# Score products with zero-padded queries on the whole TensorE array, and q and k asked for two batches ahead, in a fused attention and MLP kernel

## Chip, core and metric

The kernel runs on one core of a Trainium2 chip. The metric is device time in microseconds (us) of one execution. Engines are named as in the profile: PE (TensorE matmul), PEld (TensorE weight load), DVE (VectorE), ACT (ScalarE), POOL (GpSimd) and SP (SyncE, which here only issues DMAs).

## The reference

Longformer-style attention (8 batches, 8 heads, 576 positions, head size 64, a band of 32 to each side and 8 global positions), followed by a two-layer MLP with a softplus:

```python
scores = scale * np.matmul(q, k.transpose(0, 1, 3, 2))          # q, k, v: (8, 8, 576, 64) float32
mask = np.abs(pos[:, None] - pos[None, :]) <= 32
mask = mask | is_global[:, None] | is_global[None, :]
scores = np.where(mask, scores, -1000000000.0)
scores = scores - np.max(scores, axis=-1, keepdims=True)
attn = np.exp(scores)
attn = attn / (np.sum(attn, axis=-1, keepdims=True) + 1e-09)
attn_out = np.matmul(attn, v)
x = attn_out.transpose(0, 2, 1, 3).reshape(4608, 512)
h = x @ w_in                                                    # (512, 2048)
g = np.maximum(h, 0.0) + np.log1p(np.exp(-np.abs(h)))
out = g @ w_out                                                 # (2048, 512)
```

## The kernel before

**Units.** Each batch's 576 rows are cut into nine blocks of 64 queries; a block of all eight heads is a *unit*, so there are 72 units. The heads go in four pairs: partitions 0 to 63 belong to the pair's first head, 64 to 127 to its second. For a unit the band needs 128 keys, and 8 global keys stand between them: 136 columns (`EXT`).

A unit's work: the score products (`sc`, L621) from the queries `qx` and the keys `kx` into a PSUM tile `s`, two head pairs to a tile; masking and row maximum on DVE (`top`, L627) into `st`; the exponential on ACT (`ex`, L648) into `pe`; row sum and reciprocal on DVE (`su`, L656 to L658) into `rs`; normalising on POOL (`no`, L664) into `pn`; transposes on PE (`tp`, L674) and their copy to `pt` by ACT or DVE. Four units make a group: `val` (L717, L724) multiplies by v into `xo`, which is copied into `xT`.

In `sc` a head pair is two matmuls, each on a 64 by 64 part of the array: head 0 on the rows and columns 0 to 63, head 1 on 64 to 127. The profile writes this as `64*64`; `128*128` is the whole array, and `72*64`, `72*32` and `128*32` are other parts.

**Batches.** For each batch q and k come by one casting DMA each from POOL's queue (`load_qk`, L220) into `qn` and `kn`, v by five DMAs from SP's queue (`load_v`, L212), each two-buffered by the batch's parity. POOL casts v to `vA`, and `shift` (L443, L444) copies it by DMA to `vB`, displaced by 64 rows. PE gathers the global rows (`pick`, L463) and transposes k and q (`tk`, L505; `tq`, L513); ACT or DVE copies each result (`kev` into `kx`, `qev` into `qx`). All of these copies are made in the helper `copy`, L409. The rows of the global queries have a small attention of their own (`sg`, `mx`, `gexp`, `tg`, `lge`, `ov`, `oz`).

**MLP tiles.** Eight units (512 tokens) make an MLP tile; there are nine. `first` (L759) gives 16 PSUM tiles `h`, ACT makes the softplus `g` of each (L764), and `second` (L769) accumulates four output tiles `o`. Exponential and softplus are in different ACT tables, so the work alternates: in an *h phase* PE makes h and ACT the softplus; in an *o phase* PE makes o, while the softmax of the next tile's units runs on DVE, ACT and POOL.

**The order.** All pieces of work are handed to a planner, `_Order` (L19), with a cost for each engine that may do them, and the work that they depend on. It simulates the engines, at each step takes the piece that can begin first (then by `rank`, then by number), picks the engine, and so fixes the order on each engine. Its costs are fixed numbers; PE's costs know nothing of a change between parts of the array. For loads it keeps a clock for each of the two DMA queues: `moves` ns after a start delay of 2000, and 1000 more. The instructions then go out in that order, and each engine executes its own in order.

`AHEAD` says how many units beyond its own a tile's o phase prepares. The load of q and k for batch b is put behind the normalising of unit 0 of batch b - 1 (`T["no", (b - 1) * NJ]`) and behind that batch's `shift`. `blank_q` (L269) zeroes the places of `kx` and `qg` that are never written: for buffer 0 right after the first q load on POOL, for buffer 1 as a planned piece.

Of the kernel before, what the change touches and what calls it, by code (L numbers as in the profile page):

```python
# [18 lines left out]
class _Order:  # L19
# [4 lines left out]
    HOP = 45  # L24

    def __init__(self, slots, kinds, banks):
        self.slots = slots
        self.kinds = kinds
        self.jobs = []
        self.opened = {p: [] for p in list(slots) + list(kinds)}  # L30
        self.users = {}
        self.banks = [None] * banks
        self.bank = {}

    def add(self, cost, emit, deps=(), rank=5, opens=(), uses=(), table=None, moves=0):

        job = dict(cost=cost, emit=emit, deps=[d for d in deps if d is not None], rank=rank, opens=list(opens),
                   table=table, moves=moves, n=len(self.jobs), at=None, end=None)
        self.jobs.append(job)
        for pool, key in job["opens"]:  # L40
            self.users.setdefault(key, []).append(job)
        for key in uses:
            self.users.setdefault(key, []).append(job)
        return job
# [30 lines left out]
    def run(self, free):  # L75
# [9 lines left out]
        order = []  # L85
        table = None
        dma = dict(SP=0, POOL=0)
        while ready:
            best = None
            for j in ready:  # L90
                t0 = max([d["at"] if d["on"] in j["cost"] and (
                    d["on"] == "PE" or d["on"] == "DMA" and (not d["moves"] or not j["moves"] and d["cost"]["DMA"][0]) or d["on"] == "POOL" and d["moves"]) else d["end"] + self.HOP
                          for d in j["deps"]] or [0])
                if j["opens"]:
                    t = self.room(j["opens"])
                    if t is None:
                        continue
                    t0 = max(t0, t)
                for e in j["cost"]:
                    t = max(t0, free[e])  # L100
                    key = (t, j["rank"], j["n"])
                    if best is None or key < best[0]:
                        best = key, j, e
            if best is None:
                raise ValueError("the order is stuck")
            _, j, e = best
            t = best[0][0]
            ready.remove(j)
            step, took = j["cost"][e]
            for pool, key in j["opens"]:  # L110
                self.opened[pool].append(key)
                if pool in self.kinds:
                    ends = [(self.closed(k), n) for n, k in enumerate(self.banks)]
                    n = min(x for x in ends if x[0] is not None)[1]
                    self.banks[n] = key
                    self.bank[key] = n
            if j["table"] and j["table"] != table:
                table = j["table"]
                t += 1290
            if j["moves"]:  # L120

                mine = "POOL" if "POOL" in j["cost"] or not j["cost"][e][0] else "SP"
                other = "SP" if mine == "POOL" else "POOL"
                start = max(dma[mine], t + 2000)
                shared = min(j["moves"], max(0, dma[other] - start))
                dma[mine] = start + j["moves"] + shared
                dma[other] += shared if dma[other] > start else 0
                j["at"], j["end"] = t, dma[mine] + 1000
            else:
                j["at"], j["end"] = t, t + took  # L130
            free[e] = t + step
            j["on"] = e
            order.append(j)
            for k in after.get(j["n"], ()):
                waiting[k["n"]] -= 1
                if waiting[k["n"]] == 0:
                    ready.append(k)
# [7 lines left out]
def kernel(  # L145
# [38 lines left out]
    SUMMED = 5  # L184
    AHEAD = [1, 2, 3, 3, 3, 3, 3, 3]

# [72 lines left out]

    qx = [const([P, HP, S], BF16, f"qx{i}") for i in range(2)]  # L260
    kx = [const([P, HP, NH5, W], BF16, f"kx{i}") for i in range(2)]
# [7 lines left out]
    def blank_q(i, eng):  # L269
        eng.memset(kx[i][:, :, 0, 0:WIN].bitcast(I32), 0)  # L270
        eng.memset(kx[i][:, :, NH5 - 1, G - WIN:G].bitcast(I32), 0)
        clear(eng, qg[i][:])

    mask = const([P, NJ, EXT], BF16, "mask")
# [127 lines left out]
    def pool(n):  # L402
        return {"POOL": (n, n)}
# [11 lines left out]
    def add_load(b, which, deps):  # L415
        if which == 2:
            T["load", b, 2] = [o.add({"DMA": (100, 0)}, lambda e, x=x: load_v(b, x), deps, rank=0,
                                     opens=[("in_v", ("in", b, 2, x))], moves=1200) for x in range(NT5)]
            return
        early = [T.get(("t" + "qk"[which], b - 2, p)) for p in range(HP)]  # L420
        early += [T.get(("pick", b - 2, x)) for x in range(2)]
        T["load", b, which] = [o.add({"POOL" if b else "DMA": (880 if b else 0, 0)},
                                     lambda e: load_qk(b, which) if b else None, deps + early, rank=0, moves=4300)]

    def add_cast(b, engines):
# [19 lines left out]
        T["shift", b] = o.add({"DMA": (100, 0)}, shift, T["cast", b, 2] + early, rank=0, moves=1500)  # L445

    def add_prep(b, gate, rank):
# [38 lines left out]
        for n, ws in enumerate(steps):  # L486
            T["pick", b, n] = o.add({"PE": (460 * len(ws) + 190, 460 * len(ws) + 300)}, lambda e, ws=ws: pick(e, ws),
                                    [T["load", b, w][0] for w in ws] + [T.get(("pick", b, n - 1))], rank=4,
                                    opens=[("pick", ("pick", b)), ("gk", ("gk", b))] if n == 0 else [],
# [10 lines left out]
        for p in range(HP):  # L500
# [24 lines left out]
            def qev(e, p=p):  # L525
                copy(e, qx[i][:, p, :].rearrange("c (q r) -> c q r", r=QR),
                     PS["tq", b, p][:].rearrange("c r q -> c q r"))
            T["tk", b, p] = o.add(mm(QR, NQ), tk, [T["load", b, 1][0], *gate], rank=rank, opens=[("tk", ("tk", b, p))])
            T["kev", b, p] = o.add({"ACT": (635, 720), "DVE": (800, 880)}, kev, [T["tk", b, p], *late, *blanks["g"]],
                                   rank=3, uses=[("tk", b, p)])  # L530
            T["tq", b, p] = o.add(mm(QR, NQ), tq, [T["load", b, 0][0], *gate], rank=rank, opens=[("tq", ("tq", b, p))])
            T["qev", b, p] = o.add({"ACT": (650, 740), "DVE": (675, 750)}, qev, [T["tq", b, p], *late], rank=3,
                                   uses=[("tq", b, p)])

    PARTS = ((0, 6, WIN, 6 * G), (6, 4, 0, 4 * G - WIN))

    def add_global(b, gate, early):
# [49 lines left out]
        def oze(e):  # L587
            for p in range(HP):
# [3 lines left out]
        ready = [T["kev", b, p] for p in range(HP)] + [T["gev", b]]  # L592
        T["sg", b] = o.add({"PE": (390, 600)}, sg, ready + early, rank=3,
                           opens=[("sg", ("sg", b, 0)), ("sg", ("sg", b, 1)), ("small", ("m2", b))])
# [6 lines left out]
                            [T["tg", b], T.get(("ov", b - 2)), T.get(("blank_g", b))], rank=2, uses=[("tg", b)])  # L601
        T["ov", b] = o.add({"PE": (393, 600)}, ov, [T["lge", b], *T["cast", b, 2], T.get(("ones_g", b))], rank=3, opens=[("ov", ("ov", b))])
        old = [T.get(("val", n4)) for n4 in range(NU)
# [4 lines left out]
    def add_scores(n, gate, rank):  # L608
# [3 lines left out]
        def sc(e, x):  # L612
# [5 lines left out]
            for y in range(2):  # L618
                for h in range(2):
                    r = slice(h * D, (h + 1) * D)  # L620
                    nc.tensor.matmul(out=ps[r, y, :], lhsT=qx[i][r, x * 2 + y, j * G:(j + 1) * G],  # L621
                                     rhs=kf[r, x * 2 + y, j * W:j * W + EXT], start=True, stop=True)

# [68 lines left out]
    def add_values(n4):  # L692
# [51 lines left out]
        T["val", n4] = o.add({"PE": (1030, 1190)}, val_, ready, rank=0,  # L744
                             opens=[("xo", ("xo", n4, half)) for half in range(2)] + ([("xT", ("xT", m))] if part == 0 else []),
# [81 lines left out]
    T["select"] = setup(select_rows, {"DVE": (1174, 1260)}, [T["places"]], 5)  # L827
    T["blank_q", 1] = setup(lambda: blank_q(1, nc.gpsimd), pool(700), [], 6)
    for i in range(2):
# [23 lines left out]
    def make_batch(b, gate, rank):  # L853
# [3 lines left out]
        if b > 1:  # L857
            for w in (1, 0):
                add_load(b, w, [T["no", (b - 1) * NJ], T["shift", b - 1]])
            add_load(b, 2, [T["shift", b - 1]])  # L860
# [27 lines left out]

    for job in o.run(dict(PE=5000, ACT=2000, DVE=4700, POOL=5800, DMA=1000)):
        job["emit"](job["on"])  # L890
# [28 lines left out]
```

## Time and profile before

Three runs gave 421.93, 424.46 and 427.48 us; the median is 424.46 us. The profile is of one execution of its own.

| | |
|---|---|
| time of the profiled execution | 427.72 us |
| its span, first to last instruction | 426.0 us |
| mean granted TensorE clock | 0.984 |
| PE busy | 390.6 us, 92%, 5440 matmuls |
| DVE busy | 246.4 us, 58% |
| ACT busy | 277.4 us, 65% |
| POOL busy | 142.3 us, 33% |
| score products L621 | 576 matmuls of 64 by 64, 39.0 us busy |
| copies of q, `qx<-tq` | 18 on DVE, mean 754 ns; 14 on ACT, mean 641 ns |
| q0 (POOL's loads), share of the 16 DMA engines | 21.6% |
| q1 (SP's transfers) | 21.3% |

A busy matmul row counts its passage through the array, so rows overlap and their sum says little. The step from the start of one row to the start of the next, on the PE timeline, says what a piece costs PE. "Idle before" names what the engine waited for.

### The profile page before, as it was taken

Reading aid. Unit: us, or ns where it says so; the run is one execution under the profiler, and the core shown is the slowest. Engines: PE = TensorE matmul, PEld = TensorE weight load, DVE = VectorE, ACT = ScalarE, POOL = GpSimd, SP = SyncE. Lnnn points to the kernel's source line nnn. Section 1 sums busy time; section 2 is a strip of 40 time slices with the busy share of each in tenths; the row PEclk is TensorE's granted clock in tenths of the full one; section 3 lists DMA queues with packets and bytes.
Section 4 is the critical chain, followed back from the end, with each engine's and each line's share of the span. In section 5 each row is a group of like instructions: output and inputs, shape, how many; then the busy total and the mean of one; then the engine's idle time right before and its main releaser. Section 6 shows DMA issues by size and latency. Waiting matters only on the chain.

```text
span 426.0 us, 13459 instructions
## 1 busy us (share of the span) xinstructions
PE 390.6 (92%) x5440; PEld 205.3 (48%) x5440; DVE 246.4 (58%) x1099; ACT 277.4 (65%) x669; POOL 142.3 (33%) x249
## 2 busy tenths in 40 slices
PE   1857998999998999789996999999989999999996
PEld 1635544554455445434543455545544555445442
DVE  5698338954587449711885168835874387425011
ACT  2787568854786667747765687668665887585620
POOL 7565605810086006700463004710471044014000
PEclk9999998999999999969999999999999999999999
DMA  6997997870078204940078101960182011001011
GB/s 94 167 221 107 166 193 127 173 165 2 26 129 200 47 0 83 211 85 2 26 143 171 37 2 55 180 142 2 52 149 66 2 51 54 0 24 53 2 49 74
DMA packets 59470, 37.57 MB, mean 88 GB/s; under 512 B 42001, under 2 KB 53265, under 8 KB 59409
## 3 DMA queue, kind: packets, MB, share of 16 engines
q0 software_dynamic: 15232, 13.65, 21.6%
q1 hardware_dynamic: 44176, 23.08, 21.3%
q8 instruction: 42, 0.69, 0.7%
q14 instruction: 20, 0.16, 0.1%
HBM read 36.71 MB, written 9.44 MB: 108 GB/s over the span
## 4 chain that ended last, share of the span: by engine, by line
PE 67%; DMA 14%; DVE 7%; ACT 5%; issue 3%; POOL 3%; SPq 0%; DVEq 0%; POOLq 0%; ACTq 0%
PE h L759 29%; PE o L769 20%; DMA qn<-in_q_dram 6%; DMA kn<-in_k_dram 6%; PE s L621 4%; PE tp L674 3%; ACT pe L648 2%; DVE sm L656 2%; PE tk L505 2%; PE tq L513 2%; PE pick L463 2%; POOL pn L664 2%; DMA v<-in_v_dram 1%; PE xo L717 1%; PE xo L724 1%
## 5 line engine op out<-in xcount | busy, mean ns | idle before, releaser
L664 POOL TENSOR_TENSOR pn<-pe,rs 128x512 bf16<-128x512 f32 x72 | 74.9, 1040 | 233.7 <-DVE rs L658 98.6
L769 PE MATMUL o<-wout,g 128*128 128x512 bf16 x576 | 144.7, 381 | 0.0
L759 PE MATMUL h<-xT,win 128*128 128x512 bf16 x576 | 136.9, 386 | 0.8 <-DVE xT L409 0.6
L764 ACT ACTIVATE g<-h 128x512 bf16<-128x512 f32 x144 | 84.6, 598 | 56.4 <-PE h L759 50.6
L648 ACT ACTIVATE pe<-st,nb 128x136 f32<-128x136 f32 x288 | 93.4, 398 | 9.4 <-POOL gw L668 4.0
L627 DVE CUSTOM_DVE_ANT_0 st<-s,mask 128x136 f32<-128x136 f32 x288 | 70.6, 294 | 32.5 <-PE s L621 32.0
L759 PEld LDWEIGHTS <-win 128*128 128x128 bf16 x576 | 53.7, 99 | 62.8 <-issue 4.8
L769 PEld LDWEIGHTS <-g 128*128 128x128 bf16 x576 | 50.8, 98 | 52.3 <-issue 2.0
L656 DVE TENSOR_REDUCE sm<-pe 128x4 f32<-128x544 f32 x67 | 47.7, 712 | 10.5 <-ACT pe L648 10.2
L621 PE MATMUL s<-kx,qx 64*64 64x136 bf16 x576 | 39.0, 243 | 1.1 <-DVE qx L409 0.6
L621 PEld LDWEIGHTS <-qx 64*64 64x64 bf16 x576 | 20.9, 113 | 32.5 <-issue 26.3
L674 PE MATMUL tp<-ident_b,pn 128*128 128x128 bf16 x288 | 30.0, 232 | 6.9 <-POOL pn L664 6.7
L436 POOL CAST vA<-v 128x512 bf16<-128x512 f32 (+3 forms) x48 | 28.6, 612 | 11.5 <-DMA v<-in_v_dram 8.9
L409 DVE COPY qx<-tq 128x576 bf16<-128x576 bf16 x18 | 13.4, 754 | 31.2 <-PE tq L513 30.9
L674 PEld LDWEIGHTS <-pn 128*128 128x128 bf16 x288 | 20.4, 102 | 20.8 <-POOL pn L664 11.9
L409 ACT COPY pt<-tp 128x512 bf16<-128x512 bf16 x32 | 18.7, 585 | 13.3 <-PE tp L674 13.3
L409 DVE COPY kx<-tk 128x32 bf16<-128x32 bf16 (+1 forms) x45 | 13.1, 349 | 23.4 <-PE tk L505 23.4
L409 DVE COPY osb<-o 128x512 f32<-128x512 f32 x11 | 7.6, 690 | 32.3 <-PE o L769 32.3
L409 ACT COPY osb<-o 128x512 f32<-128x512 f32 x25 | 14.6, 585 | 16.6 <-PE o L769 12.5
L627 DVE DVE_READ_ACCUMULATOR2_ANT nb<- 128x1 f32 x288 | 23.7, 82 | 0.0
L409 DVE COPY pt<-tp 128x512 bf16<-128x512 bf16 x40 | 16.8, 421 | 11.3 <-PE tp L674 10.9
L658 DVE TENSOR_SCALAR rs<-rs,notg 128x4 f32<-128x4 f32 x72 | 19.6, 272 | 2.6
(118 smaller groups left out, 400.1 us busy)
## 6 DMA issues: line engine op xcount, KB each, us to landing
out_dram<-osb SPq DMA_DIRECT2D x36, 256.0 KB, 2.2
v<-in_v_dram SPq DMA_DIRECT2D x24, 256.0 KB, 6.1
kn<-in_k_dram POOLq DMA_DIRECT2D x8, 576.0 KB, 8.2
qn<-in_q_dram POOLq DMA_DIRECT2D x8, 576.0 KB, 12.4
vB<-vA SPq DMA_DIRECT2D x16, 256.0 KB, 4.7
v<-in_v_dram SPq DMA_DIRECT2D x16, 192.0 KB, 4.8
win<-in_moe_w_in_dram POOLq DMA_DIRECT2D x4, 512.0 KB, 9.8
wout<-in_moe_w_out_dram POOLq DMA_DIRECT2D x4, 512.0 KB, 12.1
```

The costliest lines, as they stand in the source:

```text
L409: (nc.scalar.copy if e == "ACT" else nc.vector.tensor_copy)(out, in_)
L436: nc.gpsimd.tensor_copy(to[r], at[r])
L621: nc.tensor.matmul(out=ps[r, y, :], lhsT=qx[i][r, x * 2 + y, j * G:(j + 1) * G], rhs=kf[r, x * 2 + y, j * W:j * W + EXT], start=True, stop ...
L627: nc.vector.tensor_tensor_reduce(out=PS["st", n][:, p, :], in0=PS["s", n, x][:, y, :], in1=mask[:, j, :], scale=-SCALE, scalar=3.0e38, op0 ...
L648: nc.scalar.activation(out=pe[:, p, 0:EXT], in_=PS["st", n][:, p, :], func=AF.Exp, bias=PS["nb", n][:, p:p + 1], scale=-1.0, **({"accum_ou ...
L656: nc.vector.reduce_sum(out=sm[:], in_=PS["pe", n][:, :, 0:EXT], axis=AX)
L658: nc.vector.tensor_scalar(out=rs[:], in0=rs[:], scalar1=notg[:, j:j + 1], scalar2=None, op0=OP.mult)
L664: nc.gpsimd.tensor_tensor(out=pn[:].rearrange("c p (a s) -> c p a s", a=2), in0=wide[:, :, :, 0:G], in1=rs[:].unsqueeze(2).unsqueeze(3).to ...
L674: nc.tensor.transpose(out=ps[:, p, :], in_=PS["pn", n][:, p, :], identity=ident_b[:])
L759: nc.tensor.matmul(out=h[:, :], lhsT=w_in_t[kd][:, c * P:(c + 1) * P], rhs=PS["xT", m][:, kd, :], start=(kd == 0), stop=(kd == KD - 1))
L764: nc.scalar.activation(out=t[:, :], in_=PS["h", m, c][:, :], func=AF.Softplus)
L769: nc.tensor.matmul(out=PS["o", m, ns][:, :], lhsT=PS["g", m, kf][:, ns * P:(ns + 1) * P], rhs=w_out_t[kf // 4][:, kf % 4, :], start=(kf == ...
```

## The change

1. **Score products.** `qx` becomes `qz`, with 128 columns for each block and head pair: head 0's 64 queries (zero on partitions 64 to 127), then head 1's 64 queries (zero on partitions 0 to 63). A head pair is then one matmul of the whole array with the same 136 columns: 288 instead of 576 matmuls.
2. **Copies of q.** `qev` writes the two halves separately, 64 partitions each, one instruction after the other on the same engine. Its planned cost is doubled. The zeros are written once: eight more memsets in each `blank_q`.
3. **Loads.** q and k of batch b are put behind the normalising of unit 2 of batch b - 2 instead of unit 0 of batch b - 1; the dependence on the `shift` of batch b - 1 stays. From batch 2 on, the planner takes loads and shifts to land 2 to 4 us later (`slack`).
4. **The planner's PE costs.** Jobs on a part of the array are marked `tiled` (no longer the score products); a change into or out of a part costs 95 ns.
5. **`AHEAD`** is 4 instead of 3 from the fourth tile on. POOL's start in the plan is 8300 instead of 5800.

```diff
+    SWITCH = 95
...
-                    t = max(t0, free[e])
+                    t = max(t0, free[e] + (self.SWITCH if e == "PE" and tiled and not j["tiled"] else 0))
...
+            if e == "PE":
+                if j["tiled"] and not tiled:
+                    t += self.SWITCH
+                tiled = j["tiled"]
...
-                j["at"], j["end"] = t, dma[mine] + 1000
+                j["at"], j["end"] = t, dma[mine] + 1000 + j["slack"]
...
-    AHEAD = [1, 2, 3, 3, 3, 3, 3, 3]
+    AHEAD = [1, 2, 3, 4, 4, 4, 4, 4]
...
-    qx = [const([P, HP, S], BF16, f"qx{i}") for i in range(2)]
+    qz = [const([P, HP, NJ, 2, G], BF16, f"qz{i}") for i in range(2)]
...
+        for p in range(HP):
+            eng.memset(qz[i][0:D, p, :, 1, :].bitcast(I32), 0)
+            eng.memset(qz[i][D:P, p, :, 0, :].bitcast(I32), 0)
...
-                                     lambda e: load_qk(b, which) if b else None, deps + early, rank=0, moves=4300)]
+                                     lambda e: load_qk(b, which) if b else None, deps + early, rank=0, moves=4300, slack=4000 if b > 1 else 0)]
...
-                copy(e, qx[i][:, p, :].rearrange("c (q r) -> c q r", r=QR),
-                     PS["tq", b, p][:].rearrange("c r q -> c q r"))
+                for h in range(2):
+                    r = slice(h * D, (h + 1) * D)
+                    copy(e, qz[i][r, p, :, h, :].rearrange("c j (q r) -> c j q r", r=QR),
+                         PS["tq", b, p][r].rearrange("c r (j q) -> c j q r", j=NJ))
...
-            T["qev", b, p] = o.add({"ACT": (650, 740), "DVE": (675, 750)}, qev, [T["tq", b, p], *late], rank=3,
+            T["qev", b, p] = o.add({"ACT": (1290, 1390), "DVE": (1350, 1430)}, qev, [T["tq", b, p], *late, *blanks["q"]], rank=3,
...
-                for h in range(2):
-                    r = slice(h * D, (h + 1) * D)
-                    nc.tensor.matmul(out=ps[r, y, :], lhsT=qx[i][r, x * 2 + y, j * G:(j + 1) * G],
-                                     rhs=kf[r, x * 2 + y, j * W:j * W + EXT], start=True, stop=True)
+                nc.tensor.matmul(out=ps[:, y, :], lhsT=qz[i][:, x * 2 + y, j, :, :],
+                                 rhs=kf[:, x * 2 + y, j * W:j * W + EXT], start=True, stop=True)
...
-                add_load(b, w, [T["no", (b - 1) * NJ], T["shift", b - 1]])
+                add_load(b, w, [T["no", (b - 2) * NJ + 2], T["shift", b - 1]])
...
-    for job in o.run(dict(PE=5000, ACT=2000, DVE=4700, POOL=5800, DMA=1000)):
+    for job in o.run(dict(PE=5000, ACT=2000, DVE=4700, POOL=8300, DMA=1000)):
```

Marked `tiled=True`: `pick`, `tk`, `tq`, `sg`, `ov` and `val`. The v loads get a slack of 3000 and `shift` one of 2000, from batch 2 on.

More of the change, by code (lines that the diff above doesn't have):

```diff
@@ L33, in __init__, with add @@
         self.bank = {}
-    def add(self, cost, emit, deps=(), rank=5, opens=(), uses=(), table=None, moves=0):
+    def add(self, cost, emit, deps=(), rank=5, opens=(), uses=(), table=None, moves=0, tiled=False, slack=0):
         job = dict(cost=cost, emit=emit, deps=[d for d in deps if d is not None], rank=rank, opens=list(opens),
-                   table=table, moves=moves, n=len(self.jobs), at=None, end=None)
+                   table=table, moves=moves, tiled=tiled, slack=slack, n=len(self.jobs), at=None, end=None)
         self.jobs.append(job)
@@ L86, in run @@
         table = None
+        tiled = False
         dma = dict(SP=0, POOL=0)
@@ L417, in add_load @@
             T["load", b, 2] = [o.add({"DMA": (100, 0)}, lambda e, x=x: load_v(b, x), deps, rank=0,
-                                     opens=[("in_v", ("in", b, 2, x))], moves=1200) for x in range(NT5)]
+                                     opens=[("in_v", ("in", b, 2, x))], moves=1200, slack=3000 if b > 1 else 0) for x in range(NT5)]
             return
@@ L444, in shift @@
             nc.sync.dma_start(out=vB[b % 2][64:P, :, :], in_=vA[b % 2][0:64, 1:NT5, :])
-        T["shift", b] = o.add({"DMA": (100, 0)}, shift, T["cast", b, 2] + early, rank=0, moves=1500)
+        T["shift", b] = o.add({"DMA": (100, 0)}, shift, T["cast", b, 2] + early, rank=0, moves=1500, slack=2000 if b > 1 else 0)
     def add_prep(b, gate, rank):
@@ L487, in add_prep @@
             T["pick", b, n] = o.add({"PE": (460 * len(ws) + 190, 460 * len(ws) + 300)}, lambda e, ws=ws: pick(e, ws),
-                                    [T["load", b, w][0] for w in ws] + [T.get(("pick", b, n - 1))], rank=4,
+                                    [T["load", b, w][0] for w in ws] + [T.get(("pick", b, n - 1))], rank=4, tiled=True,
                                     opens=[("pick", ("pick", b)), ("gk", ("gk", b))] if n == 0 else [],
@@ L525, in qev @@
             def qev(e, p=p):
-                copy(e, qx[i][:, p, :].rearrange("c (q r) -> c q r", r=QR),
-                     PS["tq", b, p][:].rearrange("c r q -> c q r"))
-            T["tk", b, p] = o.add(mm(QR, NQ), tk, [T["load", b, 1][0], *gate], rank=rank, opens=[("tk", ("tk", b, p))])
+                for h in range(2):
+                    r = slice(h * D, (h + 1) * D)
+                    copy(e, qz[i][r, p, :, h, :].rearrange("c j (q r) -> c j q r", r=QR),
+                         PS["tq", b, p][r].rearrange("c r (j q) -> c j q r", j=NJ))
+            T["tk", b, p] = o.add(mm(QR, NQ), tk, [T["load", b, 1][0], *gate], rank=rank, tiled=True, opens=[("tk", ("tk", b, p))])
             T["kev", b, p] = o.add({"ACT": (635, 720), "DVE": (800, 880)}, kev, [T["tk", b, p], *late, *blanks["g"]],
                                    rank=3, uses=[("tk", b, p)])
-            T["tq", b, p] = o.add(mm(QR, NQ), tq, [T["load", b, 0][0], *gate], rank=rank, opens=[("tq", ("tq", b, p))])
-            T["qev", b, p] = o.add({"ACT": (650, 740), "DVE": (675, 750)}, qev, [T["tq", b, p], *late], rank=3,
+            T["tq", b, p] = o.add(mm(QR, NQ), tq, [T["load", b, 0][0], *gate], rank=rank, tiled=True, opens=[("tq", ("tq", b, p))])
+            T["qev", b, p] = o.add({"ACT": (1290, 1390), "DVE": (1350, 1430)}, qev, [T["tq", b, p], *late, *blanks["q"]], rank=3,
                                    uses=[("tq", b, p)])
@@ L592, in add_global @@
         ready = [T["kev", b, p] for p in range(HP)] + [T["gev", b]]
-        T["sg", b] = o.add({"PE": (390, 600)}, sg, ready + early, rank=3,
+        T["sg", b] = o.add({"PE": (390, 600)}, sg, ready + early, rank=3, tiled=True,
                            opens=[("sg", ("sg", b, 0)), ("sg", ("sg", b, 1)), ("small", ("m2", b))])
@@ L601, in add_global @@
                             [T["tg", b], T.get(("ov", b - 2)), T.get(("blank_g", b))], rank=2, uses=[("tg", b)])
-        T["ov", b] = o.add({"PE": (393, 600)}, ov, [T["lge", b], *T["cast", b, 2], T.get(("ones_g", b))], rank=3, opens=[("ov", ("ov", b))])
+        T["ov", b] = o.add({"PE": (393, 600)}, ov, [T["lge", b], *T["cast", b, 2], T.get(("ones_g", b))], rank=3, tiled=True, opens=[("ov", ("ov", b))])
         old = [T.get(("val", n4)) for n4 in range(NU)
@@ L743, in val_ @@
             val(e)
-        T["val", n4] = o.add({"PE": (1030, 1190)}, val_, ready, rank=0,
+        T["val", n4] = o.add({"PE": (1030, 1190)}, val_, ready, rank=0, tiled=True,
                              opens=[("xo", ("xo", n4, half)) for half in range(2)] + ([("xT", ("xT", m))] if part == 0 else []),
@@ L827 @@
     T["select"] = setup(select_rows, {"DVE": (1174, 1260)}, [T["places"]], 5)
-    T["blank_q", 1] = setup(lambda: blank_q(1, nc.gpsimd), pool(700), [], 6)
+    T["blank_q", 1] = setup(lambda: blank_q(1, nc.gpsimd), pool(3200), [], 6)
     for i in range(2):
```

## Prediction, made before the changed kernel ran

> **What bounds the kernel now.** I read the page's busy shares first, then the PE timeline, then the table by stretches, the waits and the loads.
>
> PE is busy for 92% of the span, no other engine for more than 65%. Busy alone proves little, so I went through PE's timeline by steps, from one row's start to the next:
>
> ```profile
> 270.14 0.39 PE L674 MATMUL tp<-ident_b,pn 128*128 128x128 bf16 x4
> 270.36 0.39 PE L700 MATMUL rt<-ident_b,gw 128*128 128x128 bf16 x4
> 270.68 0.31 PE L621 MATMUL s<-kx,qx 64*64 64x136 bf16 x4
> 270.92 0.60 PE L769 MATMUL o<-wout,g 128*128 128x512 bf16 x2
> 271.45 0.30 PE L621 MATMUL s<-kx,qx 64*64 64x136 bf16 x4
> ```
>
> The four tp take 0.22 us, 0.055 each, and rt follows without a gap. The four rt take 0.32: 0.10 passes before the score products begin on their quarters of the array. The score products take 0.24. In a row of eight the second four cost 0.12 (0.35 together, at 274.12), so a lone run loses 0.12. The two o take 0.53, where two at the steady 0.216 take 0.43: again 0.10. Entering a part of the array costs PE about 0.10, leaving it as much, and the first steps after each change together about 0.03 more. PE does not idle in the waits' sense; it is simply late, and everything queued on it is late with it.
>
> ```profile
> 182.80:201.50 18.70, 18.70 (x144) 8.57 (x144) 2.68 (x14) 11.66 (x19) 0.00 (x0) 0.85 0.13 29
> 201.50:226.00 24.50, 23.87 (x379) 12.64 (x378) 20.77 (x94) 17.18 (x48) 12.63 (x20) 1.00 0.47 96
> 226.00:248.60 22.60, 19.56 (x220) 9.46 (x217) 6.43 (x33) 13.30 (x24) 2.47 (x4) 0.92 0.35 75
> 248.60:273.00 24.40, 24.40 (x425) 12.92 (x418) 20.82 (x94) 18.03 (x49) 11.02 (x18) 1.00 0.37 67
> ```
>
> This is the table by stretches: length, then PE, PEld, DVE, ACT and POOL busy, and PE's granted clock. Stretches one and three are h phases: DVE has a third of its time or less to do. Two and four are o phases: PE is full, but DVE is at 85% and ACT at 70 to 74%. So PE sets the end of an h phase, and in an o phase DVE stands right behind it. The clock of 0.85 and 0.92 is the trace of a wait just before:
>
> ```profile
> 180.17 0.63 PE L463 MATMUL pick<-qn,pick 72*32 72x128 bf16 x32 [1.42 <-DMA qn<-in_q_dram]
> ...
> 231.96 0.63 PE L463 MATMUL pick<-qn,pick 72*32 72x128 bf16 x32 [2.71 <-DMA qn<-in_q_dram]
> ```
>
> After both waits h runs at about 0.43 instead of 0.216 per matmul for some microseconds.
>
> **The change, part by part**, against the profiled execution: 427.72 us, of which 426.0 are span and 1.7 lie around it. It stands 3.3 above the median of the runs, 424.46.
>
> *Switches of the array.* I counted the rows of the PE timeline in order: 318 changes between parts of the array; 97 unbroken runs of score products. With the same order and the score products on the whole array, 144 changes are left; 174 go, 169 of them after 45 us, where PE begins to bound. After 45 us: 169 x 0.097 + 93 runs x 0.034 = 19.6 us of PE time. In h phases it is 67 changes and 37 runs, 7.8 us, and PE alone sets their end: taken whole. In o phases it is 102 changes and 56 runs, 11.8 us or 1.7 for each of seven. There I take half, 5.9, because of the copies below. Together -13.7; bounds -7.8 and -19.6.
>
> *The products themselves.* 288 matmuls of the whole array with 136 columns. The nearest row is tp with 128 columns and a 128-column weight load: 0.055 x 136/128 = 0.059 a step. A pair of quarter products takes 0.003 + 0.056 today. So 0. What hides the longer weight load is the matmul before; the load's own row is 102 ns, so without that cover 288 x (102 - 59) ns = +12.4 us. The tp row shows the cover at work, so I take 0 and keep +12.4 as a rival. The Trainium skill, "TensorE: Matmul & The Clock Gate", section "Back-to-back issue gap", gives about 81 ns for a sustained matmul of 128 columns with its own weight load; the trace has 55. By the page's figure this term would be about +6, an estimate.
>
> *Copies of q.* A copy of 64 partitions has as many elements in each partition, so it costs as much as one of 128. Two back to back on ACT take 1.18 (the timeline at 291.30), so +0.59 each on 14; on DVE 0.754 less the overlap of about 0.07, so +0.68 on 18. Together +20.5 us, 2.6 a batch, nearly all at the turn from h to o phase, where tk and tq are made. The four o phases after 201.5 last 24.5 on average, DVE 21.0, ACT 18.0. If DVE gets half of the 2.6, it has 22.3 to do; PE, without switches, about 22. So an o phase can't shrink to PE's need: from 24.5 to some 23.5, the half taken above. Without that cover the copies cost the whole 20.5. The copies made in h phases (batch 1, around 50 and 62) are hidden by DVE's idle time.
>
> *Loads.* These are the times at which each was asked for and when PE used it first:
>
> ```profile
> 165.50 0.88 POOL L220 DMA_DIRECT2D kn<-in_k_dram  x1
> ...
> 167.39 0.86 POOL L220 DMA_DIRECT2D qn<-in_q_dram  x1
> ...
> 215.20 0.88 POOL L220 DMA_DIRECT2D kn<-in_k_dram  x1
> ...
> 218.44 0.86 POOL L220 DMA_DIRECT2D qn<-in_q_dram  x1
> ```
>
> q lands 12.7 and 13.5 us after (the chain), just when pick wants it. The new gate, unit 2 of batch b - 2, lies far back, but the shift of batch b - 1 stays in the condition and now decides: SP's rows have the shifts at 82.9, 131.7, 174.3, 215.4 and 274.0. The loads of batches 3 to 7 therefore move from 119, 165, 215, 264 and 309 to about those times, 30 to 45 us ahead of their use. Their buffer was read last by tq of b - 2, long before. Each issue is 0.8 to 0.9 us on POOL, as often as before, in front of casts and pn. In the DMA queues they now meet the five v loads and the shift at the start of an h phase, when q1 has few output stores; vB, needed one phase later, may land some us later at no cost. Batch 2 moves from 71 to some 57, behind the w_out loads of the same queue.
> Gain: the waits of 1.46 and 2.77 for q and of 1.07 for k at 316; half-clock work after them, 18.7 x 0.15 + 22.6 x 0.08 = 4.6. Sum 9.9. I take -8, since R and xT are also waited for nearby (0.7 at 175.7, 0.3 at 226.9). Bounds -10 and, if another wait steps in, 0.
>
> *Start.* Sixteen memsets of 64 x 288 words. Rows of 128x320 words take 0.35, so 0.33 each, 5.3 us. POOL is idle from 10.7 to 14.5, waiting for v; so the casts begin at 16.0 instead of 14.5, and w_in, issued behind three of them at 17.46, some 1.2 later, and behind it the first k of batch 1, for which PE already waits 1.03 at 36.4. The doubled copies of batch 0 put the first exponential back by 0.7. Together +1.9; bounds 0 and 5.3.
>
> *AHEAD 4.* The tile 3 phase gets nine units (27 to 35) instead of eight. A unit is about 2.3 us of DVE (masks 0.9, sums 1.1, its share of copies 0.3). That phase lasts 28.5, of which 4.3 are waits, with DVE at 21.8: DVE then needs 25.4 with the copies. The next phase begins with no unit ready. +1.5; bounds 0 and 4. In the last tile one unit fewer stands in 376.8 to 393.6, where PE is busy for 16.8 of 16.8: no gain.
>
> *The planner* may save some of the 144 other changes by grouping: up to 20, -2; I take -1.
>
> Sum: -13.7 + 0 - 8 + 1.9 + 1.5 - 1 = -19.3, so 427.72 - 19.3 = 408.4. Some waits of this execution may be smaller in a median one, but what is taken away leaves little of them; I say 409.
>
> **The rivals.**
> 1. *DVE and ACT become the bound of the o phases.* For: DVE at 85 to 90% there, with +1.3 each. Against: its gaps are 3.5 us a phase, and PE's are smaller. Then o phases gain nothing, h phases and loads do: -7.8 - 8 + 1.9 + 1.5 + 2 (phases that grow) = -10.4, 417.
> 2. *Slower: the q copies on the path.* At the turn into an o phase every score product of the new batch waits for its copies, and DVE runs them ahead of sums and masks that feed POOL and tp. If each of the seven o phases grows by the whole 2.6 and keeps no switch gain: +18.2 - 7.8 + 1.9 + 3 (AHEAD), and loads give 0 because the softmax is what is late: +15, 443; with half of the loads' gain 439. It decides from about 2 us of growth an o phase on. Against: half of the copies go to ACT, which idles 6 to 7 us a phase.
> 3. *A whole-array product costs more than a pair*: its weight load is not covered, +12.4, so 421. Against: tp's step. The skill's "TensorEngine Tiling (Array Packing)", section "When to Use Tiling", would have a contraction of 64 on split rows for up to twice the speed. By it this change would give up 288 x 0.059 = 17 us, an estimate; but here the two quarters carry the same two heads that one padded pass carries.
> 4. *The loads don't do what is said*: they land earlier and another wait takes their place at the same turns. 409 + 8 = 417.
> 5. *All of it arrives*: -19.6 - 9.9 - 2 + 1 = -30, 397.
>
> **How the numbers follow.** Forecast (403 to 415) 0.45; rival 1 0.20; rival 2 0.08; rival 3 0.05; rival 4 0.10; rival 5 0.12. About 2% (8.5 us, below 416 or above 433) is what a measurement tells from no change. Faster takes the forecast, rival 5 and a little under half of 1 and 4: 0.70. Slower is rival 2, less a part that stays within: 0.07. Same: 0.23. The range leaves out rival 2 and part of 5 and of 3: 399 to 424.
>
> **What would show it.** Right: L621 rows `128*128` x288 with steps of 0.059 and no 0.10 around them; some 130 to 145 changes of the array; no pick waiting for q after 45 us, and clocks near 1.00 at the h phases' start; q copies on 64 partitions, x64, at unchanged mean; o phases of about 23.5 with DVE near 95%; the first h at 46 to 47 instead of 45.3. Wrong: score steps near 0.1 (rival 3); o phases as long as before with PE waiting for pn, qz or R (rivals 1 and 2); the loads still asked for within 15 us of their pick (rival 4).

## The result, and the profile after

The changed kernel takes 406.37 us (median of four runs, 402.19 to 412.03); the kernel before took 425.97 on the same chip. The ratio is 0.948, with a 95% interval of 0.933 to 0.963: faster, as forecast, and the median is 2.6 us from the predicted 409. Two of the changed kernel's four runs (409.82 and 412.03, at granted clocks of 0.983 and 0.975 instead of 0.99) and one of the kernel before are in a slower state, so this ratio compares the other runs alone (402.6 with 424.6), as all ratios below do. The profiled execution took 402.19, with a span of 400.4 and a clock of 0.990. The profiled execution of before (427.72) was above its median and this one below, so the 25.5 us between the two profiles are more than the 19.6 between the medians.

PE's timeline after; the columns are start, length, line, tiles, part of the array:

```profile
201.12 0.81 PE L779 MATMUL o<-wout,g 128*128 128x512 bf16 x3
201.77 0.40 PE L631 MATMUL s<-kx,qz 128*128 128x136 bf16 x4
202.00 0.28 PE L485 MATMUL gt<-ident_b,gk 128*128 128x128 bf16 x2
202.21 0.46 PE L596 MATMUL ov<-vA,lg 128*32 128x128 bf16 x20
```

The three o take 0.65, 0.216 each, and the score products follow at once. Four whole-array products take 0.23, so 0.058 each; gt follows at once. Only ov, on strips of 32 columns, is preceded by a pause of 0.10. Counted over the timeline, 112 changes of the array are left of 318.

The table by stretches (length; PE, PEld, DVE, ACT, POOL busy; PE's clock), an h phase, an o phase and the next h phase:

```profile
178.40:197.60 19.20, 19.20 (x262) 10.61 (x258) 15.91 (x78) 13.56 (x26) 7.40 (x12) 1.00 0.91 154
197.60:216.80 19.20, 19.01 (x327) 10.70 (x326) 13.68 (x43) 17.90 (x51) 9.99 (x15) 1.00 0.69 124
216.80:239.40 22.60, 21.67 (x333) 12.36 (x330) 14.33 (x77) 15.81 (x32) 1.49 (x4) 1.00 0.22 49
```

Before, DVE had 2.7 to 6.4 us to do in an h phase and 20.8 in an o phase. Now it has 14 to 16 in the one and 13.7 in the other. Its work has spread over the period, and the clock is 1.00 in all three. The copies of q are as dear as expected:

```profile
L419 DVE COPY qz<-tq 64x576 bf16<-64x576 bf16 x32 | 24.1, 753 | 4.8 <-PE tq L523 4.5
L419 ACT COPY qz<-tq 64x576 bf16<-64x576 bf16 x32 | 20.4, 636 | 2.9 <-PE tq L523 2.6
```

And q lies ready before it is wanted; no row of pick waits for q after the start. Here it was asked for at 138.3, and is read at 161.6:

```profile
138.26 0.81 POOL L227 DMA_DIRECT2D qn<-in_q_dram  x1
```
```profile
161.62 0.63 PE L473 MATMUL pick<-qn,pick 72*32 72x128 bf16 x32
```

I added up PE's steps from 45 us on, in the two profiles (each step against the steady step of its kind):

| us | before | after |
|---|---|---|
| changes of the array | 26.3 | 7.7 |
| slower first steps beside them | 4.8 | 2.2 |
| waits, by these steps | 19.2 | 17.0 |
| half clock after waits | 4.3 | 3.3 |
| first matmul to 45 us | 36.1 | 36.5 |

The work itself is the same within 2 us. The profile's own figure for PE's idle time from 45 us on, which begins only when the last matmul has passed through the array, is 14.4 before and 12.5 after; the runs below are compared by it. On this reading nearly all of the gain is PE's changes of the array, and the loads gave 3 us. The experiments show that this reading is wrong by itself.

### The profile page after: what moved, and what is told of

Same layout as the page of the kernel before. It is cut to its first block, busy times and chain, and to the rows that moved or that the text cites. A ratio compares the mean times of both kernels' runs of the same rounds, so it can differ in the third digit from the quotient of the medians.

```text
span 400.4 us, 12909 instructions
## 1 busy us (share of the span) xinstructions
PE 366.4 (91%) x5152; PEld 204.6 (51%) x5152; DVE 256.3 (64%) x1093; ACT 288.0 (72%) x707; POOL 146.8 (37%) x265
## 3 DMA queue, kind: packets, MB, share of 16 engines
q0 software_dynamic: 15232, 13.65, 22.3%
## 4 chain that ended last, share of the span: by engine, by line
PE 61%; DVE 16%; DMA 7%; ACT 6%; issue 5%; POOL 4%; SPq 0%; DVEq 0%; POOLq 0%; ACTq 0%
PE h L769 31%; PE o L779 15%; DMA kn<-in_k_dram 6%; DVE sm L666 5%; PE s L631 3%; PE tp L684 3%; PE tk L515 2%; DVE rs L668 2%; ACT L571 2%; PE xo L727 2%; PE tq L523 2%; DVE st L637 2%; ACT pe L658 2%; PE xo L734 2%; POOL vA L446 2%
## 5 line engine op out<-in xcount | busy, mean ns | idle before, releaser
L779 PE MATMUL o<-wout,g 128*128 128x512 bf16 x576 | 142.0, 382 | 0.0
L769 PE MATMUL h<-xT,win 128*128 128x512 bf16 x576 | 138.3, 381 | 3.5 <-issue 3.5
L779 PEld LDWEIGHTS <-g 128*128 128x128 bf16 x576 | 53.2, 98 | 50.2 <-issue 1.6
L631 PE MATMUL s<-kx,qz 128*128 128x136 bf16 x288 | 35.5, 235 | 0.9 <-ACT qz L419 0.3
L631 PEld LDWEIGHTS <-qz 128*128 128x128 bf16 x288 | 24.4, 103 | 20.7 <-issue 4.1
L684 PEld LDWEIGHTS <-pn 128*128 128x128 bf16 x288 | 19.6, 102 | 27.5 <-POOL pn L674 23.3
L419 DVE COPY osb<-o 128x512 f32<-128x512 f32 x18 | 12.4, 687 | 30.2 <-PE o L779 30.2
L419 DVE COPY qz<-tq 64x576 bf16<-64x576 bf16 x32 | 24.1, 753 | 4.8 <-PE tq L523 4.5
L668 DVE TENSOR_SCALAR rs<-rs,notg 128x4 f32<-128x4 f32 x72 | 21.2, 294 | 2.6
L419 ACT COPY qz<-tq 64x576 bf16<-64x576 bf16 x32 | 20.4, 636 | 2.9 <-PE tq L523 2.6
L727 PE MATMUL xo<-R,oz 128*32 128x256 bf16 (+3 forms) x384 | 19.2, 259 | 0.3 <-DVE R L419 0.3
```

Of the source, the lines that this page charges most:

```text
L419: (nc.scalar.copy if e == "ACT" else nc.vector.tensor_copy)(out, in_)
L631: nc.tensor.matmul(out=ps[:, y, :], lhsT=qz[i][:, x * 2 + y, j, :, :], rhs=kf[:, x * 2 + y, j * W:j * W + EXT], start=True, stop=True)
L668: nc.vector.tensor_scalar(out=rs[:], in0=rs[:], scalar1=notg[:, j:j + 1], scalar2=None, op0=OP.mult)
L684: nc.tensor.transpose(out=ps[:, p, :], in_=PS["pn", n][:, p, :], identity=ident_b[:])
L769: nc.tensor.matmul(out=h[:, :], lhsT=w_in_t[kd][:, c * P:(c + 1) * P], rhs=PS["xT", m][:, kd, :], start=(kd == 0), stop=(kd == KD - 1))
L779: nc.tensor.matmul(out=PS["o", m, ns][:, :], lhsT=PS["g", m, kf][:, ns * P:(ns + 1) * P], rhs=w_out_t[kf // 4][:, kf % 4, :], start=(kf == ...
```

## The experiments

Twelve kernels, in four groups; kernels of one group ran on one chip beside the kernel before, whose median was 425.7, 428.8, 429.5 and 428.7 there. So ratios are compared, not times.

### Which part carries the gain

*Score products alone.* Parts 1 and 2; loads, `AHEAD` and the planner's PE costs as before (POOL's start in the plan stays at 8300).

```diff
-    SWITCH = 95
-    AHEAD = [1, 2, 3, 4, 4, 4, 4, 4]
+    SWITCH = 0
+    AHEAD = [1, 2, 3, 3, 3, 3, 3, 3]
-    add_load(b, w, [T["no", (b - 2) * NJ + 2], T["shift", b - 1]])    # and no slack anywhere
+    add_load(b, w, [T["no", (b - 1) * NJ], T["shift", b - 1]])
```

> The kernel before with parts 1 and 2 alone: whole-array score products, doubled q copies, the zeros. Loads, AHEAD as before, a change of the array costs the planner nothing. Theory A (PE's changes of the array carry the gain): some 140 to 150 changes are left of 318, about 17 us of PE time go, and the time is 407 to 412, 14 to 18 under before. Theory B (the earlier loads carry half of it or more): 416 to 420, and pick still waits 3 us or more for q. Theory C (the q copies make DVE and ACT the bound without the rest of the change): 418 or more, with PE waiting for pn and R in the o phases.

Measured: 425.23 us, ratio 1.002 (0.997 to 1.007). Theory A has fallen. 144 changes are left, as it said, and the time does not move. The page's chain of work that ended last shows why (shares of the span, by engine, then by line). Before:

```profile
PE 67%; DMA 14%; DVE 7%; ACT 5%; issue 3%; POOL 3%; SPq 0%; DVEq 0%; POOLq 0%; ACTq 0%
PE h L759 29%; PE o L769 20%; DMA qn<-in_q_dram 6%; DMA kn<-in_k_dram 6%; PE s L621 4%; PE tp L674 3%; ACT pe L648 2%; DVE sm L656 2%; PE tk L505 2%; PE tq L513 2%; PE pick L463 2%; POOL pn L664 2%; DMA v<-in_v_dram 1%; PE xo L717 1%; PE xo L724 1%
```

With the score products alone:

```profile
PE 57%; DMA 21%; DVE 10%; POOL 4%; issue 4%; ACT 3%; SPq 0%; POOLq 0%; DVEq 0%; ACTq 0%
PE h L769 27%; PE o L779 17%; DMA qn<-in_q_dram 14%; DMA kn<-in_k_dram 6%; POOL pn L674 2%; PE tk L515 2%; PE tp L684 2%; DVE qz L419 2%; PE pick L473 2%; DVE st L637 2%; PE tq L523 2%; PE s L631 2%; ACT pe L658 2%; DVE sm L666 1%; PE xo L727 1%
```

The load of q now stands in the chain with 14% of the span, 60 us. Picks begin at 133.5, 180.8, 230.8, 276.8 and 322.0; before they began at 132.2, 180.2, 232.0, 278.3 and 322.4. PE does less between two picks, but the picks stay where they were. What PE saved on changes goes into idle time (24.9 us from 45 us on, against 14.4 before) and into a lower clock: the mean granted clock of the profile fell from 0.984 to 0.968. The wait of pick for q is little longer (4.9 instead of 4.1); the new ones are for `pn` (6.4), `rs` and `R`.

Theory C was met as well: over 418, with PE waiting for `pn` and `R`. The copies of q take 10 us of this chain (8.8 on DVE, 1.3 on ACT), where they took 0.8 before. With the late loads they fall at the turn from h to o phase, as the prediction's first two rivals have it. No run makes whole-array products without the second copy, so how the lost gain divides between the late loads and the copies behind them is not shown.

*Loads alone.* Part 3 in the kernel before.

```diff
-    add_load(b, w, [T["no", (b - 1) * NJ], T["shift", b - 1]])
+    add_load(b, w, [T["no", (b - 2) * NJ + 2], T["shift", b - 1]])    # and the slack of all loads and shifts
```

> The kernel before with part 3 alone: the earlier gate for q and k, and the slack. Theory A: the waits for q (4.2 us) and the half clock after them go, other waits come up at the same turns, and the time is 420 to 425, within 1.5% of before. Theory B: 414 to 418, as the waits and the half clock, 9.9 us together, are gone and nothing takes their place.

Measured: 415.51, ratio 0.984 (0.975 to 0.993). The time lies in theory B's range; the ratio, which would be 419 on the 425.7 of this chip, lies between the two. The waits for q are gone, and PE's idle time is 10.5 us. The load of q has left the chain's list, and PE's share of the chain has grown from 67% to 82%:

```profile
PE 82%; DMA 7%; DVE 4%; issue 3%; POOL 1%; ACT 0%; SPq 0%; DVEq 0%; POOLq 0%; ACTq 0%
```

PE, with 312 changes of the array, is now the bound. (They are counted on the weight loads here, since 61 matmul records are missing from this trace; the matmuls alone show 306.)

*The planner's PE cost alone.* Part 4 in the kernel before, with `sc` marked `tiled` as well.

```diff
+    SWITCH = 95        # and its two uses in run()
...
-            T["sc", n, x] = o.add(mm(2, EXT), lambda e, x=x: sc(e, x), ready + gate, rank=rank,
+            T["sc", n, x] = o.add(mm(2, EXT), lambda e, x=x: sc(e, x), ready + gate, rank=rank, tiled=True,
```

> The kernel before with part 4 alone: the planner counts 95 ns for a change of the array, with the score products marked as a part of it too. Theory A: it groups what is alike, some 240 to 280 changes instead of 318, and the time is 418 to 423. Rival (the planner's counting carries the gain, whatever the products run on): under 200 changes and 406 to 412. Second rival: grouped score products starve DVE and the time is 426 or more.

Measured: 419.17, ratio 0.985 (0.981 to 0.989); 266 changes. As theory A had it.

*The changed kernel with old loads*: the old gate and no slack, all else kept.

```diff
-    add_load(b, w, [T["no", (b - 2) * NJ + 2], T["shift", b - 1]])    # slack 2000 to 4000
+    add_load(b, w, [T["no", (b - 1) * NJ], T["shift", b - 1]])        # slack 0
```

> The changed kernel with the gate and the slack of the loads as before. Theory A: PE's waits for q come back, the stalls that the profile calls issue move with the loads, and the time is 406 to 411, at most 1.5% above the changed kernel. Theory B: 414 to 418.

Measured: 420.17, ratio 0.993 (0.989 to 0.997). Theory A said at most 411; the miss is large and on the side of theory B. There are 116 changes of the array, as few as in the changed kernel, and together with the rest they are worth 0.7%. Waits for q and k take 4.8 us again, where the changed kernel has none. Not all of the loss is theirs: pauses that the profile calls issue (see the last section) take 11.5 us, against 5.5 in the changed kernel, and this part depends on the order alone. Picks are at 132.5, 180.4, 230.3, 270.3 and 317.8.

### Two bounds side by side

The new theory, D: two chains limit the kernel, and they are nearly equal. One is PE's queue. The other goes from the first normalised unit of a batch over the load of q for the next (12 to 13.5 us), to pick, the copies of q, the next h phase and the next batch's first unit. Whoever shortens one alone meets the other.

*Score products and loads together.* In the changed kernel:

```diff
-    SWITCH = 95
-    AHEAD = [1, 2, 3, 4, 4, 4, 4, 4]
+    SWITCH = 0
+    AHEAD = [1, 2, 3, 3, 3, 3, 3, 3]
```

> Parts 1, 2 and 3 together: whole-array score products and the earlier loads with their slack; a change of the array costs the planner nothing, AHEAD as before. Theory D (two bounds side by side: PE with its array changes, and the chain from a unit's normalising over the load of q to pick; each hides what is gained on the other): 404 to 411, far under the score products alone (no gain) and the loads alone (415.5). Rival (the two parts add up, so the planner's counting and AHEAD made the rest): 414 to 418.

Measured: 404.49, ratio 0.942 (0.933 to 0.950). One part alone gives nothing, the other 1.6%, both 5.8%. This is theory D's result, and it needs neither the planner's PE cost nor `AHEAD`.

*The changed kernel with no cost of an array change:*

```diff
-    SWITCH = 95
+    SWITCH = 0
```

> The changed kernel with the planner's cost of an array change set from 95 to 0. Theory D: some 140 changes instead of 112, 3 us more PE time, 405 to 411. Rival (the planner's counting is what lets the rest through): 414 or more.

Measured: 408.00, ratio 0.953 (0.947 to 0.959), 140 changes. Against the changed kernel (0.933 to 0.963) this can't be told apart. Against the run above, which differs from it in `AHEAD` alone, it is 0.011 higher, with intervals that overlap a little: whether `AHEAD` 4 costs something stays open.

### Early, or known to be late?

Part 3 does two things: it asks earlier, and it tells the planner that loads land later. The planner had counted 2.0 + 4.3 + 1.0 us for k and another 4.3 for q behind it, so q 11.6 after the request of k. In the trace of before q lands 12.8 to 16.7 us after it, for batches 3 to 7.

*The slack without the early gate*, in the changed kernel:

```diff
-    add_load(b, w, [T["no", (b - 2) * NJ + 2], T["shift", b - 1]])
+    add_load(b, w, [T["no", (b - 1) * NJ], T["shift", b - 1]])
```

> The changed kernel with the old gate of q and k but the new slack: the planner asks for them as late as before, and knows that they land later. If the old kernels lost time because pick was placed ahead of work that PE could have done meanwhile (an error of the plan): 404 to 411. If the chain normalising, load, pick, next h phase is itself the bound (a latency): 415 to 422, with PE waiting less for q and more for other things.

Measured: 398.90, ratio 0.934 (0.926 to 0.941), below even the first range. So the load's latency as such was no bound, and theory D keeps its second chain only in this form: what bound was pick's place in PE's queue: PE executes in order, and a pick that the plan puts too early holds back all that stands behind it. In the changed kernel with old loads, pick stands in front of `val` (`xo`) and all h of the tile, and they wait with it, although `R` was ready for `val` at 177.6:

```profile
180.42 1.05 PE L473 MATMUL pick<-qn,pick 72*32 72x128 bf16 x32 [3.24 <-DMA qn<-in_q_dram]
181.25 1.07 PE L473 MATMUL pick<-kn,pick 72*32 72x128 bf16 x32
182.10 0.43 PE L727 MATMUL xo<-R,oz 128*32 128x256 bf16 x4
```

With the slack PE runs `val` and eleven h ahead of the same batch's pick, and pick finds its data:

```profile
173.46 2.75 PE L769 MATMUL h<-xT,win 128*128 128x512 bf16 x11
176.14 0.45 PE L515 MATMUL tk<-ident_b,kn 72*64 72x72 bf16 x16
176.52 0.63 PE L473 MATMUL pick<-qn,pick 72*32 72x128 bf16 x32
```

Here q had been asked for at 161.9 and landed at 172.8.

*The early gate without the slack*, in the changed kernel: all `slack` arguments taken out.

```diff
-    rank=0, moves=4300, slack=4000 if b > 1 else 0)]
+    rank=0, moves=4300)]        # likewise v (3000) and the shift (2000)
```

> The changed kernel without the slack: q and k are asked for at the new gate, but the planner takes all loads and shifts to land as early as before. If the early request alone frees pick, since the data then lies ready whatever the plan believes: 400 to 408, no wait of pick for q after 45 us. If the slack is what helps, because the plan's error also sits in v and the shift: 412 or more.

Measured: 400.75, ratio 0.938 (0.931 to 0.945), and no wait of pick for q after 45 us. Beside the other parts of the change, either half of part 3 is enough: data that lies ready forgives a wrong plan, and a right plan forgives late data.

*The slack alone in the kernel before.*

```diff
-    rank=0, moves=4300)]
+    rank=0, moves=4300, slack=4000 if b > 1 else 0)]        # likewise v (3000) and the shift (2000)
```

> The kernel before with the slack alone: quarter score products, the old gate, no cost of an array change. If the planner's error about the loads is the second bound, this frees it as the early gate did: 411 to 417, PE full of array changes as before. If the early request matters for its own sake: 421 to 427.

Measured: 421.76, ratio 0.985 (0.977 to 0.992). The time falls in the second range, but the kernel before ran at 429.5 on this chip. As ratios to the 425.7 of the first group, the ranges are 0.966 to 0.980 and 0.989 to 1.003, and 0.985 lies between them. What it does show is that the slack alone gives here what the whole of part 3 gave (0.984), and PE's wait for q falls from 4.1 us to 0.9.

### The copies of q, and an accident of order

*Every copy of q twice*, the planner told so:

```diff
-                for h in range(2):
+                for h in (0, 1, 0, 1):
...
-            T["qev", b, p] = o.add({"ACT": (1290, 1390), "DVE": (1350, 1430)}, qev,
+            T["qev", b, p] = o.add({"ACT": (2570, 2670), "DVE": (2690, 2770)}, qev,
```

> The changed kernel with every copy of q made twice, the planner told so: another 21 us of DVE and ACT work. If DVE and ACT have room, since with early loads tk, tq and these copies are spread over h and o phases: 405 to 412, under half of the added work. If the copies stand on the path at the turn into the o phases, as the second rival of the prediction has it: 420 or more.

Measured: 398.84, ratio 0.931 (0.925 to 0.937). 128 copies, 88 us of DVE and ACT instead of 44 (the expected 21 was too low by half), and the kernel is not slower; it is below the expected 405. It has room, so the prediction's second rival is excluded for the new order. For the old order it is not, as the score products alone showed.

*The larger planned cost, with each copy made once*: the second half of that diff alone.

```diff
-            T["qev", b, p] = o.add({"ACT": (1290, 1390), "DVE": (1350, 1430)}, qev,
+            T["qev", b, p] = o.add({"ACT": (2570, 2670), "DVE": (2690, 2770)}, qev,
```

> The changed kernel with the planner told that a q copy takes twice its time, while each is made once: only the order changes. If the gain of the run with doubled copies came from the order that the larger cost makes: 395 to 401. If it came by chance from where the instructions' own loads fall, with no stall put down to issue there: 402 to 410, with such stalls back.

Measured: 394.84, ratio 0.9225 (0.916 to 0.929): the fastest kernel here, ahead of the changed one with intervals that do not meet. Against the run above, which plans the same costs, 44 us of copies cost 0.9%, with intervals that overlap. The faster time comes from the order alone, and it beats both kernels.

*The same from batch 2 on only:*

```diff
+    {"ACT": (2570, 2670), "DVE": (2690, 2770)} if b > 1 else {"ACT": (1290, 1390), "DVE": (1350, 1430)}
```

> The changed kernel with the planner told that a q copy takes twice its time from batch 2 on; batches 0 and 1 are planned as in the changed kernel. With the larger cost for all batches the first h began at 50.6 instead of 46.1, while the first o began 1.3 earlier and the span was 7.5 shorter. If the gain is made in the steady tiles: 390 to 395, as the late start goes too. If it is made by the order of the start (batches 0 and 1 up to the first o): 398 to 406.

Measured: 401.02, ratio 0.934 (0.931 to 0.938). So most of the gain needs the larger cost in the first two batches. In the changed kernel, and in this one, PE stands for 2.65 us before tg, waiting for the exponential of batch 1's global rows, and once more from 92 us on:

```profile
65.80 0.71 PE L585 MATMUL tg<-ident_b,pg 128*128 128x128 bf16 x5 [2.65 <-ACT pg L571]
```
```profile
91.79 0.81 PE L769 MATMUL h<-xT,win 128*128 128x512 bf16 x3
96.13 2.29 PE L769 MATMUL h<-xT,win 128*128 128x512 bf16 x5 [3.53 <-issue]
```

That is the changed kernel. With the cost from batch 2 on it stands again:

```profile
96.47 0.59 PE L769 MATMUL h<-xT,win 128*128 128x512 bf16 x1 [3.31 <-issue]
```

With the larger cost for all batches both waits are gone; PE is busy for 21.9 of 22.0 us between 46 and 68, and for 21.8 of 22.0 between 88 and 110, against 18.7 and 18.5 in the changed kernel. The granted clock is 1.00 in that profile from end to end. The larger cost is no better estimate: it happened to give another order at the start.

Such accidents spread the results, but less than the gap that theory D is about. All eight kernels with whole-array products and at least half of part 3 lie at 0.9225 to 0.953. The two without part 3 lie at 0.993 and 1.002, and the three with quarter products at 0.984 and 0.985.

## Why the prediction was right, and where it was not

The time, the sign and the range were right. The sum behind them was not, in two steps that made up for each other, so that the time came out within 2.6 us is partly luck. Orders that differ in nothing but a planned cost ran from 0.9225 to 0.953, some 395 to 408 us.

**Switches of the array.** The count was right (174 to go with the old order; 144 left, in the run with the score products alone), and so was the price. The step that failed is the half taken off in o phases, "because of the copies": -13.7 forecast. In the profile after, 18.6 of change time and 2.6 of slow first steps are gone, 21.2 together, some 3 of it by the planner's 32 changes below. With the loads early DVE did not stand behind PE, since its work could move: it has 13.7 of 19.2 us in an o phase where 22.3 were forecast.

**The products themselves** cost nothing more, as forecast: steps of 0.058. Rival 3 is out. The Trainium skill, "TensorE: Matmul & The Clock Gate", section "Back-to-back issue gap", gives about 81 ns for a sustained matmul of 128 columns with its weight load; the trace does not agree, as whole-array products of 136 columns, each with its own weight load, step at 58 to 60 ns here in runs of two to four between other matmuls. The Trainium skill, "TensorEngine Tiling (Array Packing)", section "When to Use Tiling", splits the rows in two for a contraction of 64. Here that gives nothing, as two quarters on the diagonal, 0.059 a pair, can be one padded pass of 0.058.

**Copies of q.** The price for one was right to 5 ns (753 and 636, from 754 and 641). Counting half of their cost in the o phases was too cautious for the new order: there they cost next to nothing, as the doubled run shows. With the old loads they do stand in the chain.

**Loads.** -8 was forecast as a term of its own. The requests moved as described, though only 17 to 31 us ahead of their picks instead of 30 to 45. The waits for q are gone, but other waits took their place, at other turns: 19.2 before, 17.0 after. This is what rival 4 described, at another place. The step that failed is deeper: terms were added up that can't be added. Without part 3 the score products are worth nothing (1.002), with it over 4% (0.942 against 0.984). The prediction saw both bounds, PE's steps and q just in time, and treated the second as 4 us of waiting and some half clock. A wait that is short because the bound next to it is nearly as long says nothing of what comes when that one goes. And the prediction took the early request for what helps; the planner's picture of the load does as well.

**Start.** +1.9 forecast; the first h came 0.8 later (46.1), the first o at 67.7 instead of 67.9. Right in kind, half in size. **AHEAD**, +1.5: not settled. **The planner**, -1: 32 changes fewer, 3 us at 0.095 each, by count; in time no run shows it, as without the planner's cost the kernel can't be told from the changed one.

## What to carry to other kernels

Before adding up what each part of a change removes, ask which other chain is nearly as long: try the parts alone and together, for a part that gives nothing alone can carry the whole gain with another. In a kernel with an order written out ahead, a wait for data is as often an error of the plan as a late request; correcting the planned landing time may do as much as asking earlier. And when an order is made by a simulation of fixed costs, changes of 1 to 3% can come from the order's accidents, so such a difference is not evidence for the edit that set it off.

## What the runs showed of the hardware

A change between parts of the array cost PE 0.09 to 0.10 us into and out of a part, whichever parts they were. A run of score products on its quarters lost another 0.03 or so in the first steps after its two changes.

PE sometimes stands for 0.3 to 3.8 us with all its data there; the profile calls it issue. The fourteen profiles have 25 such pauses of over 0.3 us. Each ended 1.2 to 1.7 us after a 16 KB packet of the queue that the profile names "q8 instruction" had landed, though such stretches make up only 6% of the time. There are 42 of these packets before and 40 after, for 10880 and 10304 matmuls and weight loads, so one for every 258 or so. And all 25 pauses end at the same place in PE's program. Counting its matmuls, weight loads and semaphore instructions from the start (a missing matmul record by its weight load), the instruction after the pause is number 193 or 194 of a block of 256, counted from 0. So PE was waiting for the next piece of its own program.

Why the piece came late is less sure. The longest pause of the changed kernel falls among the loads of q and k for batch 3. This is the DMA view of 92.0 to 96.2 (packets, MB, time that the packets took as a share of the 16 DMA engines, which can pass 100% in sum):

```profile
q0 software_dynamic: 703, 0.61, 91.9%
q1 hardware_dynamic: 562, 0.14, 26.4%
q8 instruction: 1, 0.02, 1.6%
```

It reads as the program's packet standing behind the loads. That is inferred from the times: no run took the loads away from such a place on purpose. It fits that these pauses moved whenever the order did, and that four orders, the fastest among them, have none.
